# Attention beside a state-space layer: VectorE's exponential tiles copied in pairs, its single score tiles on zero-padded keys, and riders that open steps by columns

## The chip, the core and the metric

The kernel runs on one core of one Trainium2 chip. The metric is the device time of one execution in microseconds (us). TensorE is called PE, its weight loads PEld, VectorE DVE, ScalarE ACT, GpSimd POOL and SyncE (which issues most DMAs) SP, as in the profile.

## The reference

Two independent layers are computed on their own inputs of 2048 x 640, and their outputs stand side by side. Layer B, attention with 32 heads that share one key and one value head of 20 columns, carries most of the work:

```python
q = (x @ wq).reshape(B, S, H, Dh).transpose(0, 2, 1, 3)      # S 2048, D 640, H 32, Dh 20
k, v = x @ wk, x @ wv                                          # one key and value head for all
scores = einsum("bhqd,bkd->bhqk", q, k) * Dh ** -0.5
b = einsum("bhqk,bkd->bhqd", softmax(scores), v).transpose(0, 2, 1, 3).reshape(B, S, H * Dh) @ wo
# layer A: a diagonal state-space layer, complex state of 640
Bu = einsum("bld,pd->blp", x + 0j, B_bar)
for t in range(L): h = Lam_bar * h + Bu[:, t]                  # hs
a = 2 * einsum("bld,dp->blp", hs, Cmat).real + x * Dskip
out = concatenate([a, b], -1)
```

## The kernel before

**Tiles.** A block is 512 queries of four heads; there are 32 blocks. A block has 64 score tiles, one for each of 16 key groups of 128 keys (`kc`) and each of its four heads (`j`), so 2048 tiles in all (`NTILE`). A score tile is 128 keys by 512 queries in PSUM. Its exponential goes to SBUF in bf16, and a value product then multiplies it with 128 x 32 padded values (20 value columns and one of ones, which gives the softmax denominator). There is no pass for a maximum: a row in the padded query carries a bound.

**Two shapes on PE.** A score contracts over at most 32 rows, so it uses a quarter of the array's rows (`32*128` in the profile). Up to four such matmuls on four row groups, one for each head, run beside each other. I call them a row step. A value product contracts over 128 keys into 32 columns (`128*32`); four of them on four column groups, again one for each head, run beside each other: a column step. PE's instruction stream alternates between a stretch of one row step and a stretch of one to five column steps.

**Two ways to an exponential.** Most tiles go to ACT: PE fills two or three 512-column banks of one of two PSUM slots (`SC0`, `SC1`, three banks each), and ACT reads them in one `ACTIVATE` of 1024 or 1536 columns (L1530). The others go to DVE. Where ACT takes two banks of a slot, the third holds one DVE tile ("own" tile); further DVE tiles ("single" or lone tiles, `MB<-QT,KT`) go to a spare bank. DVE's exponential is made from bits: its first pass (L867, `BIG<-SC` or `BIG<-MB`) turns the score into the int16 bit pattern of a bf16 power of two, and three further copies of these 512 words, moved by 32, 64 and 96 (`SHIFTS`), are made from the first one by integer addition (POOL's `INT64_ADD`, L1858, or DVE's `TENSOR_SCALAR` on `BIG<-BIG`). The sum of the four, each with its own scaled values (`VS`), approximates the exponential. So a DVE tile needs four value products where an ACT tile needs one. Copies are made for two tiles at a time, the same shift of each, between any two of 20 (later 41) buffers of 512 words (`dhold`, `two`).

**Background.** All else on PE, the query projections, the state-space layer and the output products, is fed between these steps as column steps. A background product can also be a rider: four row pieces of it, each placed in the row group that a row step leaves free (`board`, L810). A rider opens a new step only where more than `KEEP_C` steps of the task are left.

**What sets the order.** The kernel is written by a planner in Python. Sources for each engine offer operations with priorities, a list schedule picks among them with assumed durations, and the result is a fixed instruction order for each engine with semaphores. A table (`STAGES`) sets priorities and limits anew as the count of tiles grows, `SHARE` limits DVE's part of the tiles. The order on the chip is therefore fixed; only waits vary. After a block's 64 tiles, its sums leave one PSUM bank (`pvsb<-MB`, L1925), and the reciprocals of the denominators pass through DRAM (L1980: `dn`, `rc`).

Of the kernel before, what the change touches and what calls it, by code (L numbers as in the profile page):

```python
# [445 lines left out]

class Holder:
# [20 lines left out]
class Build:  # L468
# [6 lines left out]
    MORE = 21  # L475
# [55 lines left out]
    def shared(self):  # L531
# [10 lines left out]
        shares["WO"] = ["qc"]  # L542
        shares["WOt"] = [f"BT{i}_{c}" for i in range(2) for c in range(NC)]
# [3 lines left out]
    SPREAD = 18.658  # L547
    SEEDS, REPLAYS = (169732,), 12
# [47 lines left out]
    def alloc(self, o):  # L596
# [49 lines left out]
        self.dn = sb(o, "dn", [64, 2, 32], BF16)  # L646
        self.rc = sb(o, "rc", [64, 2, 32], BF16)
# [165 lines left out]
    def board(self, op, used):  # L813
# [5 lines left out]
        for r in self.rides:  # L819
# [26 lines left out]
            return  # L846

# [22 lines left out]
    def program(self):  # L870
# [16 lines left out]
        self.dhold = [Holder(i) for i in range(self.NDS)]  # L887
# [9 lines left out]
        self.outs = 0  # L897
# [9 lines left out]
        self.s.spawn(self.more())  # L907
        self.free_banks.remove(self.pvbank)
# [32 lines left out]
    KEEP, KEEP_Q = 4200.0, 4  # L941
# [500 lines left out]
    def rules(self):  # L1442

        while self.stages and self.stages[0][0] <= self.tile_n:
# [7 lines left out]
        (0, {'STAY': 1.2, 'PAUSE': 500.0, 'pe': 192.807, 'dve': 150.0, 'KEEP_C': 3, 'OPEN': 1, 'PATIENCE': 2500.0, 'MARGIN':  # L1452
            648.138, 'WAITING': 2, 'REFILL': 905.623, 'SPARE': 148.045, 'LAG': 162.255, 'SOON': 3981.867, 'EARLIER': 3, 'LATER':
            7, 'AHEAD': 10, 'CAP': 3, 'ROOM': 4, 'ALONE': 1.397, 'TASK': 0.95, 'PV': 2.034, 'EV': 0.52, 'P1': 0.5, 'COPY': 0.569,
            'COPY1': 0.792, 'P1OWN': 0.391, 'PVEV': 0.2, 'SCARCE': 8, 'BACKLOG': 9, 'GRACE': 55.439, 'SHARE': 0.281, 'MISC_FIRST':
            0}),
        (250, {'STAY': 1.357, 'pe': 198.49, 'WAITING': 3, 'SPARE': 136.396, 'LAG': 190.385, 'SOON': 2730.774, 'EARLIER': 4,
            'ALONE': 2.237, 'PV': 1.984, 'COPY': 0.522, 'COPY1': 0.897, 'PVEV': 0.209, 'GRACE': 21.699, 'SHARE': 0.29}),
        (500, {'STAY': 1.083, 'pe': 192.807, 'PATIENCE': 2175.307, 'MARGIN': 696.79, 'SPARE': 163.248, 'LAG': 230.582, 'SOON':
            3202.285, 'EARLIER': 5, 'ALONE': 2.657, 'TASK': 0.989, 'PV': 1.9, 'P1': 0.475, 'COPY': 0.554, 'P1OWN': 0.406, 'PVEV':  # L1460
            0.2, 'SCARCE': 6, 'BACKLOG': 7, 'SHARE': 0.301}),
        (850, {'STAY': 1.2, 'PAUSE': 1035.401, 'dve': 185.73, 'PATIENCE': 2500.0, 'MARGIN': 765.584, 'WAITING': 2, 'REFILL':
            766.143, 'SPARE': 136.396, 'LAG': 240.378, 'SOON': 2255.472, 'EARLIER': 4, 'ALONE': 1.449, 'TASK': 0.95, 'PV': 1.889,
            'EV': 0.544, 'COPY': 0.57, 'PVEV': 0.259, 'BACKLOG': 9}),
        (1200, {'STAY': 0.876, 'PAUSE': 500.0, 'dve': 233.993, 'MARGIN': 696.79, 'REFILL': 905.623, 'LAG': 230.879, 'SOON':
            2154.193, 'ALONE': 2.13, 'PV': 1.756, 'EV': 0.506, 'COPY1': 0.9, 'PVEV': 0.2, 'BACKLOG': 8}),
        (1600, {'STAY': 1.2, 'PAUSE': 897.677, 'pe': 196.33, 'dve': 185.73, 'KEEP_C': 2, 'PATIENCE': 2150.555, 'WAITING': 3,
            'REFILL': 962.106, 'SOON': 2730.774, 'EARLIER': 5, 'AHEAD': 9, 'CAP': 2, 'ALONE': 1.525, 'PV': 1.9, 'COPY': 0.522,
            'PVEV': 0.309, 'BACKLOG': 7}),
    )  # L1470

    def fill_now(self, op, i, n):
# [6 lines left out]
        if s.t >= op.due or not self.can_d() or len(self.d_free()) < len(self.SHIFTS):  # L1479
            return True  # L1480
# [98 lines left out]
    def want_own(self):  # L1579
        if self.tile_n >= NTILE - self.LAST or self.d_count + 1 > self.SHARE * (self.tile_n - 16) or self.behind():  # L1580
            return False
        if sum(1 for o in self.firsts if o.start is None) >= self.WAITING:
            return False
        self.firsts = [o for o in self.firsts if o.start is None]
        return len(self.d_free()) > len(self.SHIFTS) - 1
# [100 lines left out]
    def can_d(self):  # L1686
# [5 lines left out]
        if b > self.pv_b and len(self.d_free()) < self.ROOM + min(self.due_copies(), self.CAP):  # L1692
            return False
# [5 lines left out]
    def due_copies(self):  # L1699
        return sum(len(d[2]) for d in self.d_open if d[3] <= self.pv_b)  # L1700

    def want_d(self, taken=0, own=0):
        s = self.s
        if self.tile_n >= NTILE - self.LAST or self.d_count + taken + own + 1 > self.SHARE * (self.tile_n - 16):
# [3 lines left out]
        return len(self.d_free()) > taken + own + len(self.SHIFTS) - 1  # L1708

    def d_source(self):  # L1710
# [9 lines left out]
        return Op("pe", [], self.mmt(512), prio=self.ALONE, mode="S", load=128.0, hook=hook)  # L1720
# [8 lines left out]
    def task_prio(self):  # L1729
        return self.TASK if self.started else 3  # L1730
# [10 lines left out]
    def fill_d(self, op, m, bank=None):  # L1741
# [6 lines left out]
        h = self.d_free()[0]  # L1748
        self.d_count += 1
        b, kc, j = self.score(op, m, bank.tensor, bank)  # L1750
        n = len(self.SHIFTS)
        h.taken, h.left, h.users = True, n, []
        key = f"DR{h.index}"
        first = self.dve(self.ts(self.dr(h.index), bank.ap, 16256.0, 0.0, ALU.add, ALU.max), 645, deps=[op],
# [5 lines left out]
        self.d_open.append([h, first, list(range(1, n)), b, kc, j])  # L1760
        self.d_left[b, j] += n - 1
        self.pv_entry(b, kc, j, 0, h, first)
# [3 lines left out]
    def pv_entry(self, b, kc, j, k, h, op):  # L1766
        self.pvq[b][j].append((self.VS[:, k], kc, self.dr(h.index, BF16), f"DR{h.index}", op, h, "VS"))
# [5 lines left out]
    def two(self, x):  # L1773
        a, b = (self.dr_at[i] for i in x)
        return bass.AP(tensor=self.BIG, offset=a, ap=[[self.BIG.shape[1], 128], [b - a, 2], [1, 512]])

    def more(self):
# [3 lines left out]
        self.dhold += [Holder(self.NDS + i) for i in range(self.MORE)]  # L1781
# [4 lines left out]

    def copy_source(self):

        s = self.s
        can = [d for d in self.d_open if d[1].end is not None and s.seen(d[1], "dve") <= s.t]  # L1790
        if not can:
            return None
        n = len(self.d_free())
        if n < 1:
            return None
        if sum(len(d[2]) for d in can) < self.BACKLOG and not (can[0][3] == self.pv_b and self.pv_filled[self.pv_b] == self.pv_need[self.pv_b]):
            return None
        k = can[0][2][0]
        two = [d for d in can if k in d[2]][:2 if n >= 2 else 1]
        if self.short(two):  # L1800
            two = two[:1]
        one = len(two) == 1
        if one and any(d[1].end is None or d not in can for d in self.d_open):
            prio = self.COPY1
        else:
            prio = self.COPY
        if can[0][3] == self.pv_b != LASTB and self.pv_filled[self.pv_b] == self.pv_need[self.pv_b]:
            prio = self.CLOSE
        return Op("dve", [], 210 if one else 342, prio=prio, port=True, hook=lambda op: self.copy(op, k, two))

    def short(self, two):

# [860 lines left out]
```

## Time and profile before

| | before |
|---|---|
| median of 3 runs (lowest, highest) | 697.5 us (696.67, 699.1) |
| span of the profiled execution, first to last instruction | 695.9 us |
| PE busy, share of the span | 683.2 us, 98% |
| ACT busy | 681.8 us, 98% |
| DVE busy | 637.0 us, 92% |
| POOL busy | 470.4 us, 68% |

Which of the runs was profiled isn't told, so the execution's own time stands for its span: 695.9 us, 0.8 us under the fastest run and 1.6 us under the median. "Busy" counts the time in which at least one instruction of the engine was under way; on ACT and PE instructions overlap, so that an instruction's mean duration is longer than the distance to the next one.

### The profile page before, as it was taken

The page shows a single profiled execution, that of the slowest core. Times are in us where ns is not written, and L with a number is a line of the kernel's source. Part 1 is how long each engine was busy: PE and PEld are TensorE (multiplying, and loading weights), DVE is VectorE, ACT ScalarE, POOL GpSimd, SP SyncE. Part 2 cuts the span into 40 slices and gives each one's busy share as a digit, 9 for nine tenths or more (in the row PEclk, how much of TensorE's full clock was granted, in tenths as well). Part 3 has the DMA queues.
Part 4 walks back from the last instruction along what each step waited for, and adds up shares of the span by engine and source line. Part 5 has one row for each costly group of instructions (what it writes and reads, how often), then busy time and mean ns, then how long its engine had stood idle before and what let it go on. Part 6 is the DMA issues. An engine that isn't in the chain of part 4 may idle for free.

```text
span 695.9 us, 27390 instructions
## 1 busy us (share of the span) xinstructions
PE 683.2 (98%) x11488; PEld 250.6 (36%) x11490; DVE 637.0 (92%) x1243; ACT 681.8 (98%) x703; POOL 470.4 (68%) x796
## 2 busy tenths in 40 slices
PE   8999999999999999999999999999999999999998
PEld 5322332334334333333433333334333332343335
DVE  7899999999999889999999999999999999977795
ACT  7999999999999999999999999999999999999996
POOL 4256666564587668767778777676776767788880
DMA  9659641211130111102110101131000001110001
GB/s 217 175 127 187 139 103 39 62 26 32 30 94 13 32 27 27 35 21 29 44 26 22 28 27 28 35 58 20 13 15 12 20 15 36 37 29 22 21 15 41
DMA packets 77591, 34.48 MB, mean 50 GB/s; under 512 B 58350, under 2 KB 77470, under 8 KB 77470
## 3 DMA queue, kind: packets, MB, share of 16 engines
q1 hardware_dynamic: 76650, 32.57, 20.3%
q8 instruction: 92, 1.51, 0.9%
q10 hardware_dynamic: 820, 0.16, 0.1%
q14 instruction: 29, 0.24, 0.1%
HBM read 11.53 MB, written 9.75 MB: 31 GB/s over the span
## 4 chain that ended last, share of the span: by engine, by line
PE 56%; ACT 42%; DVE 1%; issue 0%
ACT PR L1530 41%; PE MB L1946 21%; PE MB L800 14%; PE SC L1626 10%; PE MB L810 8%; PE MB L730 1%; DVE BIG L867 1%; PE SC L1162 1%; PE SC L726 1%; PE MB L726 0%; ACT L2197 0%; PE SC L730 0%; DVE pvsb L1925 0%; PE MB L1279 0%; DVE QT L867 0%
## 5 line engine op out<-in xcount | busy, mean ns | idle before, releaser
L1530 ACT ACTIVATE PR<-SC 128x1024 bf16<-128x1024 f32 (+1 forms) x678 | 666.6, 1131 | 4.5 <-PE SC L1626 3.3
L1858 POOL INT64_ADD BIG<-BIG x761 | 458.1, 617 | 198.1 <-DVE BIG L867 54.7
L867 DVE TENSOR_SCALAR BIG<-SC 128x512 int16<-128x512 f32 x560 | 376.2, 684 | 38.7 <-PE SC L1626 33.1
L1946 PE MATMUL MB<-BIG,VS 128*32 128x512 bf16 (+1 forms) x2468 | 269.8, 376 | 1.2 <-DVE pvsb L1925 0.9
L1626 PE MATMUL SC<-QT,KT 32*128 32x512 bf16 (+1 forms) x2073 | 265.3, 378 | 4.4 <-ACT PR L1530 1.8
L1946 PE MATMUL MB<-PR,VP 128*32 128x512 bf16 (+1 forms) x1495 | 222.3, 378 | 0.1
L1626 PEld LDWEIGHTS SC<-QT,KT 32*128 32x128 bf16 x2073 | 67.3, 91 | 133.8 <-ACT PR L1530 77.1
L1946 PEld LDWEIGHTS MB<-BIG,VS 128*32 128x32 bf16 x2468 | 68.5, 95 | 65.5 <-issue 41.4
L1946 PEld LDWEIGHTS MB<-PR,VP 128*32 128x32 bf16 x1495 | 55.1, 94 | 45.8 <-issue 33.0
L867 DVE TENSOR_SCALAR BIG<-BIG 128x1024 int16<-128x1024 int16 (+1 forms) x136 | 52.3, 419 | 0.9 <-PE MB L1946 0.4
L800 PE MATMUL MB<-CA,W 128*32 128x320 bf16 (+2 forms) x992 | 51.4, 299 | 0.4 <-DVE BIG L2366 0.4
L810 PE MATMUL MB<-xaT,BT 32*128 32x256 bf16 x192 | 37.1, 273 | 0.0
L800 PE MATMUL MB<-CT,W 128*32 128x512 bf16 (+1 forms) x640 | 36.0, 302 | 0.6 <-issue 0.6
L800 PE MATMUL MB<-xaT,BA 128*32 128x256 bf16 x800 | 31.8, 275 | 0.0
L810 PE MATMUL MB<-diagD,xaT 32*128 32x128 bf16 x320 | 31.3, 217 | 0.0
L810 PEld LDWEIGHTS MB<-diagD,xaT 32*128 32x128 bf16 x320 | 17.7, 92 | 29.1 <-ACT PR L1530 17.7
L800 PEld LDWEIGHTS MB<-CA,W 128*32 128x32 bf16 x992 | 22.8, 96 | 14.2 <-issue 5.7
L800 PE MATMUL MB<-xaT,BT 128*32 128x256 bf16 x608 | 26.2, 274 | 0.0
L2133 DVE CAST stg<-MB 128x512 bf16<-128x512 f32 x35 | 23.8, 680 | 1.8 <-PE MB L800 1.1
L862 DVE TENSOR_TENSOR prod<-MB,tab 128x1024 bf16<-128x1024 f32 x20 | 24.3, 1215 | 0.2
L867 DVE TENSOR_SCALAR BIG<-MB 128x512 int16<-128x512 f32 x35 | 23.8, 679 | 0.6 <-PE MB L1626 0.6
L2406 DVE TENSOR_TENSOR_SCAN g<-sc,hst,prod 128x256 bf16<-128x256 f32 x30 | 22.5, 749 | 0.0
(178 smaller groups left out, 502.4 us busy)
## 6 DMA issues: line engine op xcount, KB each, us to landing
out_dram<-stg SPq DMA_DIRECT2D x33, 128.0 KB, 2.0
qd<-BIG SPq DMA_DIRECT2D x20, 128.0 KB, 2.1
QT<-qd SPq DMA_DIRECT2D x28, 80.0 KB
OP<-pvsb SPq DMA_DIRECT2D x105, 20.0 KB
rdP<-recs SPq DMA_DIRECT2D x105, 20.0 KB
lbd<-BA SPq DMA_DIRECT2D x5, 320.0 KB, 2.7
CT<-in_B_x_dram SPq DMA_DIRECT2D x2, 640.0 KB, 5.3
BA<-in_A_B_re_dram SPq DMA_DIRECT2D x1, 800.0 KB, 7.5
```

The costliest lines, as they stand in the source:

```text
L726: r = e.matmul(out[32 * j:32 * j + 32], lhsT=lhsT[:, 32 * j:32 * j + 32], rhs=rhs, start=start, stop=stop, tile_position=(0, 32 * j), skip ...
L730: return lambda e: e.matmul(out, lhsT=lhsT, rhs=rhs, start=start, stop=stop, **kw)
L800: x = e.matmul(out[32 * j:32 * j + 32], lhsT=lhsT[:, 32 * j:32 * j + 32], rhs=rhs, start=start, stop=r.end is tag, tile_position=(0, 32 * ...
L810: return lambda e: e.matmul(out, lhsT=lhsT[at], rhs=rhs[at], start=start, stop=r.end is tag, tile_position=(32 * row, 0), skip_group_check ...
L862: return lambda e: e.tensor_tensor(out, a, b, op)
L867: return lambda e: e.tensor_scalar(out, a, s1, s2, op0=op0, op1=op1)
L1530: ex = self.act(lambda e: e.activation(dst, t[:, 0:512 * n], ACT.Exp, scale=1.0 / UNIT), 0.8333 * 512 * n + 64, table="exp", deps=[op], re ...
L1626: r = e.matmul(out[:, bank.off + lo:bank.off + lo + n], lhsT=p.KT[32 * j:32 * j + 32, 128 * c:128 * c + 128], rhs=p.QT[32 * j:32 * j + 32, ...
L1858: op.fns.append(lambda e: e.int64_add(words(dst), words(src), add))
L1946: r = e.matmul(bank.tensor[32 * j:32 * j + 32, bank.off + at:bank.off + at + n], lhsT=v[:, c, 0:32], rhs=rhs[:, lo:lo + n], start=first an ...
L2133: ev = self.dve(lambda e: e.tensor_copy(st, bank.ap), 645, deps=[prev], reads=[bank.key], writes=[key], prio=self.EV, gate=(lambda: last.e ...
L2406: o = self.dve(lambda e, ri=ri, init=init: e.tensor_tensor_scan(p.g[:, u, ri, :], rdec, p.prod[:, 1, 0, ri, :], init, ALU.mult, ALU.add), ...
```

## The change

The diff rewrites the handling of DVE's tiles and retunes the planner's table.

- **Pairs.** Buffers are held as pairs of neighbours (10, later 20 pairs). Two DVE tiles share a pair. The pair's first copy (shift 32) is one operation on 1024 words; the other two (64 and 96) are one operation on 2 x 1024 words, since adding 64 to the tiles and to their first copy gives both (`CHAIN`, `step_of`).
- **Lone tiles on zero-padded keys.** After the last row of queries is projected, POOL zeroes four strips of 384 columns in `BIG` and SP copies 32 rows of the last three key groups into each (`lone_keys`). A single tile of these key groups is then scored by four `128*32` matmuls that contract over all 128 rows, three quarters of them zeros in the keys (`lone`, `MB<-QT,BIG`), a column step.
- **Riders.** A rider opens a step where at least `RIDE_N` columns of the task's other steps are left (654 to 2600, by stage), in place of a count of steps.
- **Also.** The reciprocal works on 128 x 16 in place of 64 x 32; a task of the output waits until `wo` has landed and a unit of the state-space layer until its inputs nearly have; tasks get a lower priority unless one is due (`EASY`); `STAGES` has 31 rows in place of 6, with another seed.

```diff
-    MORE = 21
+    MORE = 20
...
-            if best is None and rows and len(r.steps) > self.KEEP_C and len(r.open) < self.OPEN:
+            if best is None and rows and len(r.open) < self.OPEN and self.width(r.steps) >= self.RIDE_N:
...
+        if self.lone_at() is not None:
+            return Op("pe", [], self.mmt(512, 4), prio=self.ALONE2, mode="C", load=512.0, hook=self.lone)
...
+            op.fns += [lambda e, i=i: e.matmul(out[32 * i:32 * i + 32, bank.off:bank.off + 512], lhsT=keys[:, at + 32 * i:at + 32 * i + 32],
+                                               rhs=p.QT[:, b % 12, :], start=True, stop=True, tile_position=(0, 32 * i),
+                                               skip_group_check=True) for i in range(4)]
...
+    def step_of(self, d, free, eng):
+
+        s = self.s
+        if d.first is not None and len(d.todo) == 2 and len(d.tiles) == 2 and self.CHAIN:
+            if d.first[1].end is None or s.seen(d.first[1], eng) > s.t:
+                return None
+            if free > 1 and not self.short(d, 4):
+                return (2, 3)
+        if free < 1 or self.short(d, len(d.tiles)):
+            return None
+        return (d.todo[0],)
...
-        two = [d for d in can if k in d[2]][:2]
-        if len(two) < 2 or self.short(two):
+        can = [x for x in self.ready_pairs("pool") if len(x[0].tiles) == 2]
+        if not can:
             return None
...
+            op.fns.append(lambda e: e.int64_add(b.bitcast(I64), a.bitcast(I64), by * 0x0001000100010001))
...
-        o = self.dma(lambda e: e.dma_start(p.dn[:, slot, :], sums.rearrange("j (s n) -> (j s) n", n=32)), 4096, dn, land=self.LATE_DMA, deps=[o],
+        o = self.dma(lambda e: e.dma_start(p.dn[:, slot, :], sums.rearrange("j (s n) -> (j s) n", n=16)), 4096, dn, land=self.LATE_DMA, deps=[o],
...
     def o_ready(self, qb):
         blks = range(NC if qb < NQB - 1 else 1)
+        if not self.s.done([self.wo_op]):
+            return False
```

How the two programs' instructions count out (the order as built; "full columns" means 512):

| instructions | before | after |
|---|---|---|
| ACT exponentials of 1024, of 1536 columns | 579, 98 | 552, 120 |
| DVE first passes (own from SC, single from MB) | 560 + 35 = 595 | 535 + 48 = 583 |
| DVE copies `BIG<-BIG`, of 512 words (15 absolute values among them) / of 2 tiles / of 4 | 24 / 127 / 0 | 18 / 17 / 9 |
| POOL `INT64_ADD` on `BIG`, of 2 tiles / of 4 | 761 / 0 | 284 / 277 |
| PE stretches of row steps, of them with a score step for ACT | 674, 672 | 668, 666 |
| row stretches with all four row groups in use / with three | 360 / 301 | 297 / 353 |
| PE column steps, in units of four matmuls of full columns | 1649 | 1683 |
| of these: value products / lone tiles / fillers on zeros (L730, `MB<-KT,VZ`) | 958 / 0 / 18.5 | 949 / 22 / 25.5 |
| background in column steps, same units | 673 | 687 |
| single tiles as row matmuls of full columns | 31 | 26 |

The PE order at a place in the second half, before: three score matmuls (own tile among them), the single DVE tile on the fourth row group, then value products.

```order
L1626 MATMUL SC<-QT,KT 128x512 x3
L1626 MATMUL MB<-QT,KT 128x512
L1946 MATMUL MB<-PR,VP 32x512
L1946 MATMUL MB<-BIG,VS 32x512
L1946 MATMUL MB<-PR,VP 32x512 x2
L1946 MATMUL MB<-BIG,VS 32x512
```

And after, at a like place, where the score lines are L1677, the value products L2106 and the lone tile L1909:

```order
L1677 MATMUL SC<-QT,KT 128x512 x3
L1909 MATMUL MB<-QT,BIG 32x512 x4
L2106 MATMUL MB<-BIG,VS 32x512 x2
L2106 MATMUL MB<-PR,VP 32x512
L2106 MATMUL MB<-BIG,VS 32x512
```

The single tile has moved from the row step into the column stretch, as a step of its own. POOL's queue before, all additions over two tiles (`2x256` are two buffers apart, `512` two neighbours, in 64-bit words):

```order
L1858 ISA BIG<-BIG 128x2x256 x3
L1858 ISA BIG<-BIG 128x512 x2
L1858 ISA BIG<-BIG 128x2x256 x2
L1858 ISA BIG<-BIG 128x512 x2
L1858 ISA BIG<-BIG 128x2x256 x3
```

And after, the additions over two tiles and over four in turn:

```order
L2007 ISA BIG<-BIG 128x512
L2007 ISA BIG<-BIG 128x2x512
L2007 ISA BIG<-BIG 128x512
L2007 ISA BIG<-BIG 128x1024
L2007 ISA BIG<-BIG 128x512
L2007 ISA BIG<-BIG 128x2x512
```

What took three POOL instructions for two tiles takes two, the second of them twice as wide. DVE's queue before had copies between its first passes:

```order
L867 TENSOR_SCALAR BIG<-SC 128x512
L867 TENSOR_SCALAR BIG<-BIG 128x1024
L867 TENSOR_SCALAR BIG<-SC 128x512 x2
L1980 RECIPROCAL rc<-dn 64x32
L867 TENSOR_SCALAR BIG<-SC 128x512
L2133 CAST stg<-MB 128x512
```

And after, in the middle of the program, mostly none:

```order
L883 TENSOR_SCALAR BIG<-SC 128x512
L2140 RECIPROCAL rc<-dn 128x16
L878 TENSOR_TENSOR W<-prod 128x2x256
L883 TENSOR_SCALAR BIG<-SC 128x512 x2
L878 TENSOR_TENSOR prod<-prod 128x512
L883 TENSOR_SCALAR BIG<-SC 128x512 x3
```

The copies have left DVE for POOL's wider instructions.

More of the change, by code (lines that the diff above doesn't have):

```diff
@@ L1799, in copy_source @@
[L1799 to L1807, printed above, removed]
+        d, ks = can[0]
+        closing = d.b == self.pv_b and self.pv_filled[self.pv_b] == self.pv_need[self.pv_b]
@@ L1836, in act_source @@
             return None
[L1837 to L1858 removed]
+        can = self.ready_pairs("act")
```

330 lines of the change are left out of this document (226 added, 104 removed).

## The prediction

> **What bounds the kernel now.** I read the page's engine line and chain first, then the groups by shape, then the window from the first exponential to the last.
>
> ```profile
> PE 683.2 (98%) x11488; PEld 250.6 (36%) x11490; DVE 637.0 (92%) x1243; ACT 681.8 (98%) x703; POOL 470.4 (68%) x796
> PE 56%; ACT 42%; DVE 1%; issue 0%
> 18.40:687.00 668.60, 661.20 (x11210) 237.77 (x11212) 620.83 (x1183) 665.93 (x677) 462.26 (x769) 1.00 0.19 44
> L1530 ACT ACTIVATE PR<-SC 128x1024 bf16<-128x1024 f32 x579 | 544.7, 1068 | 4.3 <-PE SC L1626 3.3 <-PE MB L1626 0.3 <-PE MB L1946 0.2
> L1530 ACT ACTIVATE PR<-SC 128x1536 bf16<-128x1536 f32 x98 | 141.6, 1505 | 0.1
> ```
>
> PE and ACT are both at 98%, and the chain of waits is shared between them (56% and 42%). The third line is the stretch that matters, 668.6 us from the first exponential to the last; its columns are PE, PEld, DVE, ACT and POOL busy, then the granted clock, 1.00. Ahead of it lie 18.4 us and behind it 695.9 - 687.0 = 8.9 us. ACT's recorded idle time, 4.5 us in that stretch, understates its waiting, because an `ACTIVATE` that waits overlaps its predecessor in the record. So I take the distance between starts where ACT doesn't wait. These four rows are single instructions of its timeline:
>
> ```profile
> 456.19 1.04 ACT L1530 ACTIVATE PR<-SC 128x1024 bf16<-128x1024 f32 x1
> 465.22 1.17 ACT L1530 ACTIVATE PR<-SC 128x1024 bf16<-128x1024 f32 x1
> 167.86 1.53 ACT L1530 ACTIVATE PR<-SC 128x1536 bf16<-128x1536 f32 x1
> 175.84 1.19 ACT L1530 ACTIVATE PR<-SC 128x1024 bf16<-128x1024 f32 x1
> 456.19 9.29 ACT L1530 ACTIVATE PR<-SC 128x1024 bf16<-128x1024 f32 x10
> ```
>
> Ten exponentials of 1024 lie between 456.19 and 465.22 (last row): 0.903 us each. Six of 1536 lie between 167.86 and 175.84: 1.330 us each. Without any wait ACT needs 579 x 0.903 + 98 x 1.330 = 522.8 + 130.3 = 653.2 us of the 668.6. Its whole slack is 15.4 us, 2.3%.
>
> PE in the same way, from a place where nothing seems to hold it (only starts matter):
>
> ```profile
> 300.34 0.39 PE L1626 MATMUL SC<-QT,KT 32*128 32x512 bf16 x3
> 300.66 0.40 PE L1946 MATMUL MB<-BIG,VS 128*32 128x512 bf16 x4
> 300.88 0.38 PE L1946 MATMUL MB<-PR,VP 128*32 128x512 bf16 x1
> 301.21 0.39 PE L1626 MATMUL SC<-QT,KT 32*128 32x512 bf16 x3
> 301.53 0.39 PE L1946 MATMUL MB<-PR,VP 128*32 128x512 bf16 x1
> 302.30 0.39 PE L1626 MATMUL SC<-QT,KT 32*128 32x512 bf16 x3
> ```
>
> A column step takes 0.22 us (300.66 to 300.88), a stretch of two 0.55 (300.66 to 301.21) and of three 0.77 (301.53 to 302.30). So a column stretch costs 0.11 plus 0.22 for each step, and a row step 0.32, of which 0.1 is again the turn to the other shape. Row step and two column steps make 0.87, under ACT's 0.903; with three they make 1.09, and ACT waits. So the two engines take turns as the bound from one exponential to the next.
>
> **The change, part by part.**
>
> *ACT.* 27 exponentials of 1024 go and 22 of 1536 come, since DVE takes 583 tiles in place of 595: -27 x 0.903 + 22 x 1.330 = -24.4 + 29.3 = **+4.9 us**, on the path wherever ACT is the bound.
>
> *PE, lone tiles.* 22 of them become column steps, 22 x 0.22 = +4.8 us. What they cost as row matmuls shows here:
>
> ```profile
> 453.17 0.39 PE L1946 MATMUL MB<-BIG,VS 128*32 128x512 bf16 x4
> 453.49 0.39 PE L1626 MATMUL SC<-QT,KT 32*128 32x512 bf16 x3
> 453.50 0.38 PE L1626 MATMUL MB<-QT,KT 32*128 32x512 bf16 x1
> 453.81 0.39 PE L1946 MATMUL MB<-BIG,VS 128*32 128x512 bf16 x1
> ```
>
> The single tile starts 0.01 us behind its three neighbours on the fourth row group, and the next stretch starts 0.32 after the row step: it was free. In the order all 31 stand in a stretch that has a score step anyway. At worst a single tile comes alone after the row step and costs another 0.32. I take free.
>
> *PE, riders.* The background needs 687 - 673 = 14 more column units, as pieces that rode on free row groups do so no longer: +3.1 us. The 12 fewer DVE tiles save 9 units of value products, -2.0. Six fewer turns of shape and row steps save 6 x (0.32 + 0.11) = -2.6. The fillers' 7 units more (+1.5) are issued where PE has nothing else, so I leave them out. PE's sum is 4.8 + 3.1 - 2.0 - 2.6 = **+3.3 us** (+4.8 with the fillers). The turn is also where a rule speaks for the change.
>
> ```profile
> PEld SC L1626 <- ACT PR L1530: 77.1, 189, 0.7
> PEld SC L1626 <- DVE BIG L867: 31.3, 77, 0.7
> PEld SC L1626 <- issue: 14.7, 42, 0.5
> ```
>
> These are the idle times of the weight queue ahead of score steps: 0.41 us each where ACT came last, 0.41 where DVE came last, 0.35 where nothing held it but the turn itself. The Trainium skill ("TensorEngine Tiling (Array Packing)", Key Properties) says that a change of tiling mode drains TensorE; the trace agrees, at 0.1 us a turn. By that rule alone, had the 22 tiles stood in stretches of their own, they would have cost 0.32 + 0.11 = 0.43 each, the new shape would bring 22 x (0.22 - 0.43) = -4.6 in place of +4.8, and PE's sum would be -6.1 (ACT's 4.9 would stand); the order has no such stretches, so the saving isn't there to be had. The same page's Performance Considerations take contractions of 32 rows as a case for row tiling, which speaks against the zero-padded keys, and the rows above agree.
>
> *DVE.* The pairs take its copies away and the shorter reciprocal some more:
>
> ```profile
> L867 DVE TENSOR_SCALAR BIG<-SC 128x512 int16<-128x512 f32 x560 | 376.2, 684 | 38.7 <-PE SC L1626 33.1
> L867 DVE TENSOR_SCALAR BIG<-BIG 128x1024 int16<-128x1024 int16 x127 | 50.2, 427 | 0.9 <-PE MB L1946 0.4
> L1980 DVE RECIPROCAL rc<-dn 64x32 bf16<-64x32 bf16 x30 | 10.0, 333 | 0.0
> L1858 POOL INT64_ADD BIG<-BIG x761 | 458.1, 617 | 198.1 <-DVE BIG L867 54.7 <-PE MB L1946 22.1 <-DVE g L2406 19.3
> ```
>
> Copies over two tiles 110 x 0.427 = -47; nine over four tiles, each between one and two of these, +3.8 to +7.7, I take +6; first passes 12 x 0.684 = -8; half the reciprocal's work between 0 and -10, I take -5 since half of its columns remain. DVE falls by some 54 us, to 583 (84%). That is off the path, except where DVE came last ahead of a score step: 77 x (0.41 - 0.35) = 4.6 us at most. ACT waits just as long there, so most of these would only change their releaser. I take **-1.2**, and keep 0 and -4.6 as ends.
>
> *POOL.* 284 additions over two tiles at 0.617 make 175 us. The 277 over four aren't in the trace: not under one of 0.617, not over two of them, so 171 to 342 us. The two memsets below, 526 ns for 512 columns and 1805 for 2048, leave a fixed part of about (4 x 526 - 1805) / 3 = 100 ns; by that a four-tile addition takes 2 x 0.617 - 0.1 = 1.13 us, 313 us in all, and POOL's copying rises to 488 us from 458. It had 198 us of idle time ahead of these instructions, which hides that and the four new memsets (narrower than QT's at 526 ns).
>
> ```profile
> L1014 POOL MEMSET QT<- 128x512 bf16 x10 | 5.3, 526 | 7.1 <-DVE M L866 4.7 <-DVE VS L862 1.8
> PEld MB L1946 <- POOL BIG L1858: 10.2, 45, 0.3
> L1017 POOL MEMSET VS<- 128x2048 bf16 x1 | 1.8, 1805 | 0.0
> SPq L1982 <- DVE rc L1980: 92.5, 25, 7.2
> SPq L1973 <- DVE BIG L867: 80.1, 20, 9.6
> ```
>
> If the cover went, a value product would find its copy late by up to one more 0.617. Today PE waits for POOL 45 times for 0.23 us, which is the ordinary gap. I take nothing; the upper end, one full 0.617 at each of 31 block ends, is 19 us, since one PSUM bank holds the sums of one block at a time.
>
> *SP.* Four loads more for the keys, and 60 small transfers in twice the rows. SP waits with an instruction for DVE for many us (last two rows) while nothing on PE stops for it; its output transfers are as many as before. Nothing, unless a copy to the keys is late, and then single tiles keep the old shape. The new conditions for `wo` and the inputs can only move background work.
>
> *Sum.* ACT-bound stretches grow by 4.9, PE-bound ones by 3.3 to 4.8. The engines are used in turn, so I take ACT's 4.9 with DVE's -1.2 against it: +3.7. From the profiled execution 695.9 + 3.7 = 699.6 us of span; the median lies 1.6 above the span, so **701.2 us**.
>
> **Rivals.**
>
> *The waits shrink by more than the work grows (faster).* The new table has 31 stages, and DVE is freer, so single and own banks come free sooner. ACT's slack is 15.4 us; if half of it went, 695.9 + 4.9 - 7.7 = 693.1 of span and 694.7 us. It decides from a slack of 15.4 - 4.9 = 10.5 us downward. For it: the slack is made of many small misfits of the order (0.87 against 0.903 against 1.09), which another order could fit better. Against it: PE has no more than 668.6 - 661.2 = 7.4 us without a matmul under way, and gets more work too. The floor without any wait is 18.4 + 658.1 + 8.9 = 685.4 of span.
>
> *No difference.* The slack shrinks by about what is added: 697.5, within 2.1 us either way. A difference of 0.3%, 2.1 us, is about what this kernel's runs can tell.
>
> *POOL's wide copies come late (slower still).* The pair has to wait for its second tile, then for a copy of twice the width; if a third of the upper end's 19 us falls on the path, 701.2 + 6.3 = 707.5. It decides once POOL's queue is longer than the value products' reserve at a block's end. Against it: POOL's 198 us idle. The Trainium skill ("SBUF — State Buffer", Who interferes with whom) says that GpSimd and a two-port VectorE instruction exclude each other for a whole instruction, so a wider POOL copy would hold VectorE longer as well; the trace agrees as far as POOL waited 54.7 us for VectorE's L867, and no run here shows the reverse.
>
> **How the numbers follow.** Forecast (699.6 to 705.7) 0.47; faster 0.28; no difference 0.15; late copies 0.10. So slower holds 0.57 against 0.28 and 0.15. The likeliest case is 701.2. For 8 in 10 the range leaves out half of the late copies and somewhat less than half of the faster case, those in which more than half of the slack goes: 692 to 706.5. The likeliest case's own range is 699.6, where no difference begins, to 705.7, where ACT's 4.9 and PE's 3.3 would both count in full and DVE's part for nothing.
>
> **What the changed profile would show.** ACT: 552 and 120 exponentials at 0.903 and 1.330 between starts, and a stretch from first to last of 671 to 674 us. If it is under 668, the slack fell below 10.5 us and the first rival holds. PE: `MB<-QT,BIG` with a start 0.22 us ahead of the next column step. DVE: under 600 us busy. POOL: the mean of four-tile additions between 0.62 and 1.23 us; if over 1.23, or if PE's waits for POOL rise from 10.2 to over 20 us, the third rival holds. The prediction would be wrong if the order of steps matters more than their number.

## The result and the profile after

| | before | after |
|---|---|---|
| median (lowest, highest), 4 runs each | 697.45 us (696.67, 699.1) | 702.93 us (702.28, 703.12) |
| ratio to before, 95% interval | | 1.0073 [1.0058, 1.0088] |
| the profiled execution, and its span | 695.9 us of span | 703.12 us, 701.2 us of span |

The changed kernel is 0.7% slower, some 5.1 us by the ratio. First the answers to the prediction's first fence: the engine line, the chain by engine, the window from the first exponential to the last (PE, PEld, DVE, ACT, POOL busy, then clock and DMA), and ACT's two groups.

```profile
PE 686.9 (98%) x11567; PEld 252.9 (36%) x11567; DVE 612.8 (87%) x1124; ACT 686.3 (98%) x698; POOL 470.6 (67%) x600
ACT 56%; PE 40%; DMA 2%; DVE 1%; issue 0%
18.25:692.52 674.27, 664.57 (x11297) 240.10 (x11298) 597.41 (x1066) 670.34 (x672) 462.50 (x573) 1.00 0.18 44
L1581 ACT ACTIVATE PR<-SC 128x1024 bf16<-128x1024 f32 x552 | 522.1, 1084 | 5.4 <-PE SC L1677 5.0 <-PE MB L2106 0.2
L1581 ACT ACTIVATE PR<-SC 128x1536 bf16<-128x1536 f32 x120 | 173.5, 1518 | 0.2 <-PE MB L2106 0.2
```

The stretch grew from 668.6 to 674.3 us, which is all of the loss between these two executions; the head is 0.15 shorter and the tail 8.7 in place of 8.9. ACT and PE stand at 98% as before, and the chain has moved from PE towards ACT. DVE lost 24 us of busy time, and the span grew all the same.

Busy time says little about two engines whose instructions overlap in the record, so I add up what each had to do in that stretch. For ACT that is the count of exponentials by the distance between starts without a wait (0.903 and 1.330 us; the quartiles of these distances are the same in both traces). For PE I take every step by the usual shortest distance of its kind to the next step (the fifth percentile over both traces: a full column step to a column step 0.215 us, column to row and row to column 0.320, narrower ones less). Depending on how neighbouring matmuls are put together into steps, the difference in PE's work comes out between 5.1 and 5.6 us.

| from the first exponential to the last, us | before | after | difference |
|---|---|---|---|
| length | 668.6 | 674.3 | +5.7 |
| ACT's work | 653.2 | 658.1 | +4.9 |
| ACT's rest | 15.4 | 16.2 | +0.8 |
| PE's work | 635.5 | 640.6 | +5.1 |
| PE's rest | 33.1 | 33.7 | +0.6 |

Both engines were given about 5 us more to do, and neither waits less than before. The two rests come from single executions, though, and the four runs of the kernel before spread over 2.4 us. That is the first reading of the loss; the experiments ask whether it holds as a cause.

A lone tile in its new shape, four matmuls on zero-padded keys (first column start, second duration, us):

```profile
325.32 0.39 PE L1677 MATMUL SC<-QT,KT 32*128 32x512 bf16 x3
325.64 0.40 PE L1909 MATMUL MB<-QT,BIG 128*32 128x512 bf16 x4
325.86 0.39 PE L2106 MATMUL MB<-BIG,VS 128*32 128x512 bf16 x4
```

It starts 0.22 us ahead of the next column step. Of the 22, 16 are followed by a column step at once and take 0.215 to 0.227 us, one more only after 0.38; the other five stand last in their stretch.

The waits (in order: total us, times, longest), the weight queue ahead of score steps and of value products, and DVE's first passes ahead of their scores:

```profile
PEld SC L1677 <- ACT PR L1581: 108.5, 264, 1.2
PEld SC L1677 <- DVE BIG L883: 27.0, 66, 1.1
PEld SC L1677 <- issue: 16.3, 46, 0.4
DVE BIG L883 <- PE SC L1677: 58.6, 166, 2.6
PEld MB L2106 <- POOL BIG L2007: 11.8, 49, 0.7
```

DVE comes last ahead of a score step 66 times in place of 77, ACT 264 times in place of 189. The 11 steps that no longer wait for DVE can be at most a small part of the 75 that now wait for ACT. The time that the pairs took off DVE shows again as waiting for PE: the first passes' idle time behind score steps went from 33.1 (the group's row before) to 58.6 us.

DVE's and POOL's groups, those that changed:

```profile
L883 DVE TENSOR_SCALAR BIG<-SC 128x512 int16<-128x512 f32 x535 | 361.1, 686 | 65.0 <-PE SC L1677 58.6 <-PE MB L1677 1.8
L883 DVE TENSOR_SCALAR BIG<-MB 128x512 int16<-128x512 f32 x48 | 32.6, 678 | 1.2 <-PE MB L1909 0.8 <-PE MB L1677 0.2
L883 DVE TENSOR_SCALAR BIG<-BIG 128x1024 int16<-128x1024 int16 x17 | 7.6, 444 | 0.4
L883 DVE TENSOR_SCALAR BIG<-BIG 128x2048 int16<-128x2048 int16 x9 | 6.3, 703 | 0.5 <-PE MB L2106 0.3
L2140 DVE RECIPROCAL rc<-dn 128x16 bf16<-128x16 bf16 x30 | 7.2, 241 | 0.0
L2007 POOL INT64_ADD BIG<-BIG x561 | 456.8, 823 | 201.4 <-DVE BIG L883 47.6 <-DVE g L2566 24.2 <-PE MB L2106 18.6
```

POOL's additions over two and over four tiles share the last row; single ones of its timeline tell them apart:

```profile
302.72 0.61 POOL L2007 INT64_ADD BIG<-BIG  x1 [4.36 <-DVE BIG L883]
303.70 1.04 POOL L2007 INT64_ADD BIG<-BIG  x1 [0.37 <-DVE prod L878]
```

A four-tile addition takes 1.04 us, so POOL copies as long as before (456.8 and 458.1 us).

### The profile page after: what moved, and what is told of

It reads as the page before. It is cut to its first block, busy times and chain, and to the rows that moved or that the text cites. A ratio compares the mean times of both kernels' runs of the same rounds, so it can differ in the third digit from the quotient of the medians.

```text
span 701.2 us, 27176 instructions
## 1 busy us (share of the span) xinstructions
PE 686.9 (98%) x11567; PEld 252.9 (36%) x11567; DVE 612.8 (87%) x1124; ACT 686.3 (98%) x698; POOL 470.6 (67%) x600
## 4 chain that ended last, share of the span: by engine, by line
ACT 56%; PE 40%; DMA 2%; DVE 1%; issue 0%
ACT PR L1581 56%; PE MB L2106 13%; PE MB L809 11%; PE SC L1677 8%; PE MB L819 4%; DMA mrep<-mab 2%; PE MB L739 1%; PE SC L1179 1%; PE SC L735 0%; DVE BIG L883 0%; DMA mcol<-mrep 0%; PE MB L735 0%; ACT L2357 0%; PE SC L739 0%; DVE prod L878 0%
## 5 line engine op out<-in xcount | busy, mean ns | idle before, releaser
L2007 POOL INT64_ADD BIG<-BIG x561 | 456.8, 823 | 201.4 <-DVE BIG L883 47.6
L883 DVE TENSOR_SCALAR BIG<-SC 128x512 int16<-128x512 f32 x535 | 361.1, 686 | 65.0 <-PE SC L1677 58.6
L1677 PE MATMUL SC<-QT,KT 32*128 32x512 bf16 (+1 forms) x2064 | 263.1, 377 | 6.6 <-ACT PR L1581 4.7
L2106 PE MATMUL MB<-BIG,VS 128*32 128x512 bf16 (+1 forms) x2408 | 263.8, 377 | 0.4 <-issue 0.4
L2106 PE MATMUL MB<-PR,VP 128*32 128x512 bf16 (+1 forms) x1510 | 215.5, 378 | 0.0
L1677 PEld LDWEIGHTS SC<-QT,KT 32*128 32x128 bf16 x2064 | 66.6, 91 | 158.7 <-ACT PR L1581 108.5
L2106 PEld LDWEIGHTS MB<-BIG,VS 128*32 128x32 bf16 x2408 | 66.1, 95 | 64.7 <-issue 42.0
L2106 PEld LDWEIGHTS MB<-PR,VP 128*32 128x32 bf16 x1510 | 53.5, 94 | 41.1 <-issue 29.0
L819 PE MATMUL MB<-xaT,BT 32*128 32x256 bf16 x176 | 34.0, 273 | 0.0
L883 DVE TENSOR_SCALAR BIG<-MB 128x512 int16<-128x512 f32 x48 | 32.6, 678 | 1.2 <-PE MB L1909 0.8
L819 PE MATMUL MB<-diagD,xaT 32*128 32x128 bf16 x320 | 31.3, 217 | 0.8 <-ACT PR L1581 0.8
L2566 DVE TENSOR_TENSOR_SCAN g<-sc,hst,prod 128x256 bf16<-128x256 f32 x30 | 24.4, 818 | 0.1
L809 PE MATMUL MB<-BIG 128*32 128x512 bf16 x300 | 22.6, 382 | 0.0
```

The source lines that it names most:

```text
L809: x = e.matmul(out[32 * j:32 * j + 32], lhsT=lhsT[:, 32 * j:32 * j + 32], rhs=rhs, start=start, stop=r.end is tag, tile_position=(0, 32 * ...
L819: return lambda e: e.matmul(out, lhsT=lhsT[at], rhs=rhs[at], start=start, stop=r.end is tag, tile_position=(32 * row, 0), skip_group_check ...
L883: return lambda e: e.tensor_scalar(out, a, s1, s2, op0=op0, op1=op1)
L1677: r = e.matmul(out[:, bank.off + lo:bank.off + lo + n], lhsT=p.KT[32 * j:32 * j + 32, 128 * c:128 * c + 128], rhs=p.QT[32 * j:32 * j + 32, ...
L2007: op.fns.append(lambda e: e.int64_add(b.bitcast(I64), a.bitcast(I64), by * 0x0001000100010001))
L2106: r = e.matmul(bank.tensor[32 * j:32 * j + 32, bank.off + at:bank.off + at + n], lhsT=v[:, c, 0:32], rhs=rhs[:, lo:lo + n], start=first an ...
```

## The experiments

Theory W: the order after the change asks for more work of ACT and PE, the two engines at the bound, the waits stay as they are, and the work is the loss. Theory O: added work would be absorbed by the waits, and the loss comes from the new order or from a new wait. Theory P, the prediction's third rival: POOL's wide copies come late. All kernels below keep the instruction order of the kernel that they start from, so that nothing is planned anew; only a_lone_moved moves 18 matmuls and, where one would come too early, the first pass that reads it. Ratios go against the kernel before, run in turn with them on the same chip; differences in us are differences of ratios by 698 us, with the intervals combined by their squares.

| kernel | changed by | median, us | ratio to before, 95% interval | against its own start, us |
|---|---|---|---|---|
| after | | 702.93 | 1.0073 [1.0058, 1.0088] | |
| b_act | before, ACT +4.2 us | 699.84 | 1.0018 [1.0009, 1.0028] | +1.3 ± 0.7 |
| b_pe | before, PE +3.2 to 3.7 | 702.63 | 1.0066 [1.0048, 1.0083] | +4.6 ± 1.2 |
| b_both | before, both | 702.66 | 1.0064 [1.0049, 1.0079] | +4.5 ± 1.0 |
| b_act_short | before, ACT -4.8 | 697.24 | 0.9982 [0.9973, 0.9991] | -1.3 ± 0.6 |
| b_pe_short | before, PE -3.0 | 696.60 | 0.9970 [0.9959, 0.9981] | -2.1 ± 0.8 |
| a_act_short | after, ACT -4.7 | 701.53 | 1.0039 [1.0027, 1.0051] | -2.4 ± 1.3 |
| a_pe_short | after, PE -3.0 | 701.79 | 1.0046 [1.0030, 1.0062] | -1.9 ± 1.5 |
| a_both_short | after, both | 698.16 | 1.0004 [0.9995, 1.0013] | -4.8 ± 1.2 |
| a_lone_moved | after, 18 lone tiles on row steps | 703.41 | 1.0068 [1.0052, 1.0084] | -0.3 ± 1.5 |
| a_lone_inplace | after, lone tiles as rows in place | 702.52 | 1.0067 [1.0054, 1.0080] | -0.4 ± 1.4 |
| a_pool_split | after, POOL +61 | 709.72 | 1.0168 [1.0152, 1.0184] | +6.6 ± 1.5 |
| a_pool_short | after, POOL -41 | 702.57 | 1.0064 [1.0046, 1.0083] | -0.6 ± 1.7 |

### Adding the work to the kernel before

Small copies between ACT's exponentials, and value products on zeros as extra column steps, 45 and 15 of them, spread evenly.

```diff
+                x = Op("act", [lambda e: e.activation(p.tscr[:], p.lift[:, 2:3], ACT.Copy)], 100.0)
...
+                op.fns[:0] = [lambda e, j=j: e.matmul(bank.tensor[32 * j:32 * j + 32, bank.off:bank.off + 512], lhsT=p.VZ[:], rhs=p.KT[:, 0:512],
+                                                      start=False, stop=False, tile_position=(0, 32 * j), skip_group_check=True) for j in range(4)]
```

> The kernel before in its own order, with 45 one-column ACT copies put evenly between its exponentials, ahead of the next exponential's wait; at the 0.11 us that two small ACT instructions stand apart they are 4.9 us of ACT work, as much as the change adds. Theory W (the work: the change is slower because its order asks more of ACT and PE, and the waits stay as they are): 700.4 to 702.4 us, 3 to 5 over before. Theory O (the order: the added work alone would vanish in ACT's 15.4 us of slack, and the change is slower because its order fits worse): under 699 us.

> The kernel before in its own order, with 15 column steps on zeros put evenly among the value products, 0.22 us each, 3.3 us of PE work. Theory W: 699 to 700.8 us, 1.5 to 3.3 over before. Theory O: under 698.5 us.

> The kernel before with both additions, 4.9 us of ACT work and 3.3 us of PE work. Theory W: 702 to 704.5 us, about the 702.9 of the changed kernel. Theory O: under 700 us.

One such copy on ACT's timeline of b_act:

```profile
299.60 1.03 ACT L1546 ACTIVATE PR<-SC 128x1024 bf16<-128x1024 f32 x1
300.50 0.21 ACT L558 ACTIVATE tscr<-lift 128x1 f32<-128x1 f32 x1
300.59 14.34 ACT L1546 ACTIVATE PR<-SC 128x1024 bf16<-128x1024 f32 x15
```

It holds ACT for 0.093 us from start to start (300.50 to 300.59, rounded), whatever its recorded 0.21, so 45 of them are 4.2 us. Of these 1.3 came out at the end: short of theory W's 3 to 5, and by this difference within the 1.5 that theory O left. PE's 15 steps are 3.2 us at 0.215 each; the sum over steps puts the same 15 at 3.7 us in b_pe and 4.3 in b_both, so it is good to about 1 us. They cost 4.6 us, their length or more and over the 1.5 to 3.3 that was expected. Both additions together, within theory W's range, cost no more than PE's alone. So the kernel before is held by PE more than by ACT, and 4.2 us of ACT and 3.2 to 4.3 us of PE give it +4.5 us, close to what the change lost.

### Taking work away, from both kernels

Every exponential behind the first 200 tiles leaves out 10 columns of its last tile, or every value product behind the first of a block 8 of its 512 columns, or both.

```diff
+        self.n_seen = getattr(self, "n_seen", 0) + n
+        cut = 512 * n - (10 if self.n_seen > 200 else 0)
+        dst = p.PR.rearrange("p a b -> p (a b)")[:, 512 * h.index:512 * h.index + cut]
...
+                n -= 8 if n == 512 and not first else 0
```

> The changed kernel in its own order, with ScalarE's work made shorter: every exp behind the first 200 key tiles leaves out the last 10 columns of its last tile (10 x 0.83 ns each, some 600 exps, about 5.0 us less work; those columns keep what an earlier exp left). Theory W (the order of the changed kernel asks for 4.9 us more of ScalarE, and ScalarE is its bound): it comes 3 to 5 us under the changed kernel, 698 to 700, about where the kernel before stands. Theory O (the exps' waits set the end, whatever the work): 1.5 us or less under it, 701.5 or more.

> The changed kernel in its own order, with TensorE's work made shorter: every value product that is not the first of its block streams 504 of 512 columns (8 columns at 0.417 ns, about 890 steps of four side by side, about 3.0 us less work; the last 8 columns of each sum lack those products). Theory W with ScalarE as the bound of the changed kernel, as the moved lone tiles suggest: 0 to 1.5 us under the changed kernel, 701.5 to 703. If TensorE is the bound after the change too: 2 to 3 us under it, about 700.

> The kernel before in its own order, with ScalarE's work made shorter in the same way (the last 10 columns of every exp behind the first 200 key tiles left out, about 5.0 us). The added copies cost 0.2 to 0.6 of their length here, so TensorE holds the exps back: 0.5 to 2 us under the kernel before, 695.5 to 697.5. If ScalarE were its bound as well: 3 to 5 us under it, about 693.

> The kernel before in its own order, with TensorE's work made shorter in the same way (504 of 512 columns in the value products behind the first of a block, about 3.0 us). TensorE is its bound: 2 to 3 us under the kernel before, 694.5 to 696. If ScalarE and TensorE hold each other up at single places only: under 1.5 us.

> The changed kernel in its own order with both cuts at once: 10 columns less in the last tile of every exp behind the first 200 key tiles (4.8 us of ScalarE), 504 of 512 columns in the value products behind the first of a block (3.0 us of TensorE). The single cuts gave 0.0034 and 0.0027 of the time before, 2.4 and 1.9 us. If each engine holds the other up at places of its own, the two add up: 4.3 us under the changed kernel, 699.0 to 700.0, a ratio of 1.001 to the kernel before. If both cuts shorten the same waits: 2.5 to 3 us, 700.5 or more. If one engine takes over as soon as the other is cut: 5.5 us or more, 698 or less.

On ACT a cut exponential starts the next one 0.008 us sooner (0.895 for 0.903, 1.322 for 1.330), 579 times in the changed kernel and 585 times in the one before, so 4.7 and 4.8 us. ACT's cut gives 2.4 us in the changed kernel and 1.3 in the one before; PE's gives 1.9 and 2.1. By these differences a_act_short and a_pe_short each fell between their two expectations; the cuts of the kernel before came as expected. So neither engine is the bound by itself, before or after. ACT's part may have grown with the change, as the chain has it, but the two intervals of ACT's cuts overlap. With both cuts the changed kernel is where the kernel before is, 1.0004 [0.9995, 1.0013], and 4.8 us are near the sum of the single cuts, 4.3, which speaks for each engine holding the other up at places of its own; the interval, 3.6 to 6.0, excludes cuts that shorten the same waits, but not the 5.5 us or more of one engine taking over from the other. Its engine line and chain:

```profile
PE 683.5 (98%) x11565; PEld 253.0 (36%) x11567; DVE 612.9 (88%) x1124; ACT 682.8 (98%) x698; POOL 470.4 (68%) x600
ACT 49%; PE 45%; DMA 3%; DVE 1%; SPq 1%; issue 0%
```

The changed kernel has kept its order, its pairs, its wide copies and its DVE queue there; only 4.7 us of ACT and 3.0 us of PE are gone, and with them the loss. Together with b_both, which gives the kernel before about the same loss by adding such work, this bears theory W out from both sides. Theory O fails in its first half: the kernel before absorbs most of ACT's added work but none of PE's, and 7.7 us taken from the two engines of the changed kernel give 4.8 back. Its second half, that the new order costs or gains something by itself, is not tested by these runs; it can only be bounded by how well the added work accounts for the loss (below).

### The lone tiles

The change's own column steps, undone in two ways: 18 of the 22 as row matmuls on the free row group of the next score step (the other four find none), or all 22 as row matmuls where they stand.

```diff
+        op.fns = [lambda e: e.matmul(out[:, bank.off:bank.off + 512], lhsT=p.KT[32 * j:32 * j + 32, 128 * kc:128 * kc + 128],
+                                     rhs=p.QT[32 * j:32 * j + 32, b % 12, :], start=True, stop=True, tile_position=(32 * j, 0))]
```

> The changed kernel with 18 of its 22 lone tiles taken out of the column stretches and put, as row matmuls on the real keys, on the free row group of the next score step; all else stays in its order. PE loses 18 column steps of 0.22 us, 4.0 us. Theory W: 699 to 701 us, 2 to 4 under the changed kernel's 702.9. Theory O, or the tiles as a thing that only fills PE's gaps: 702 to 703.5 us. If the later score holds up VectorE or the next fill: over 703.5 us.

> The changed kernel in its own order, with the 22 lone tiles at their places as single 32-row matmuls instead of zero-padded column steps: each then lies as a row between two column steps and costs two more turns, 22 x 0.21 us = 4.6 us more of TensorE at just these places. If TensorE's time at these places is on the path, as the prediction's sum had it (0.6 to 1 of it by what the other cuts gave): 2.8 to 4.6 us over the changed kernel, 706 or more. If ScalarE is the bound there, as the moved lone tiles suggest: 0 to 1 us, 703 to 704.5.

Moved, the tiles take 3.9 us off PE by the sum over steps, and the time stays: theory W's 2 to 4 us under the changed kernel did not come. The chain of a_lone_moved shows what may be a part of the reason:

```profile
PE 57%; ACT 33%; DVE 5%; DMA 3%; issue 0%; POOL 0%; POOLq 0%
```

DVE stands at 5% in place of 1%. A lone tile that is scored later reaches DVE later: DVE's first passes wait 4.1 us for the moved tiles, 9 times, where they waited 0.8 us for the lone tiles of the changed kernel. That this is what eats up PE's 3.9 us is not shown, but it makes the run a poor test of the steps' own price. The second run was to add 4.6 us of turns at the same places, and didn't: 18 of the 22 have a row step right ahead or behind and join it, and PE's sum fell by 2.4 us. In the trace, 12 of these 18 row stretches still last 0.45 to 0.65 us, not much less than row step and zero-padded step together (0.32 + 0.22), so little of that sum was saved in fact; the time didn't move either. So the shape of the lone tile is worth nothing that can be measured here, one way or the other. What a step at these places costs by itself, these two runs leave open, and theory W rests on work that was added and taken away evenly over the kernel, not on the change's own steps.

### GpSimd's copies

The wide additions split into two of two tiles, or all additions 140 columns short of each pair.

```diff
+                one = [(self.wide_at([x], n), self.wide_at([y], n)) for x, y in zip(free, src)]
+                op.fns += [lambda e, o=o, i=i: e.int64_add(o.bitcast(I64), i.bitcast(I64), by * 0x0001000100010001) for o, i in one]
...
+            if all(h.index in self.full for h in free):
+                a, b = self.wide_at(src, n, 140), self.wide_at(free, n, 140)
```

> The changed kernel in its own order, with each of GpSimd's 277 four-tile additions made as two of two tiles: 277 x (2 x 0.588 - 1.013) = 45 us more of GpSimd, 457 to about 502 us. If the copies' time on GpSimd is on the path (the prediction's third rival): 2 to 5 us over the changed kernel, 705.5 or more. If not: 0 to 1 us. By the way VectorE's operations on SBUF: if they wait for the end of one GpSimd addition, their mean falls back (prod<-prod 526 to some 440 ns) because each is shorter; if they wait by GpSimd's total, it stays or grows.

> The changed kernel in its own order, with GpSimd's copies made shorter: behind the first copy into each buffer an addition leaves out the last 140 columns of each pair of tiles (884 of 1024, 1768 of 2048; at 0.415 ns a column of each pair some 0.058 us a pair, 838 pairs, about 45 us less of GpSimd, 457 to about 412; those columns keep an older copy). The split additions cost 6.6 us for 65 us more of GpSimd. Theory P (the wide copies come late as the change stands, and a part of its 5.2 us is theirs): 2 to 5 us under the changed kernel, 698 to 701. Theory W (the change's loss is ScalarE's and TensorE's work, and GpSimd has slack up to about where it stands): 0 to 1 us under it, a ratio of 1.006 or more to the kernel before.

The groups of additions and the chain in a_pool_split (L2009 are the split ones):

```profile
L2009 POOL INT64_ADD BIG<-BIG x554 | 344.3, 635 | 46.9 <-POOL BIG L2011 13.3 <-DVE g L2570 4.2 <-DVE BIG L883 3.8
L2011 POOL INT64_ADD BIG<-BIG x284 | 177.8, 630 | 101.3 <-DVE BIG L883 33.4 <-DVE CT L878 14.7 <-DVE diagD L882 11.5
PE 58%; ACT 23%; POOL 7%; DVE 6%; issue 3%; DMA 2%; POOLq 0%; DVEq 0%
```

And in a_pool_short its group, and PE's waits for it:

```profile
L2010 POOL INT64_ADD BIG<-BIG x561 | 415.5, 748 | 241.2 <-DVE BIG L883 59.5 <-PE MB L2110 26.8 <-DVE g L2570 25.4
PEld MB L2110 <- POOL BIG L2010: 10.2, 41, 1.0
```

The two groups overlap where one addition follows another; POOL's engine line rose from 470.6 to 531.3 us, by 61. With that POOL enters the chain with 7% and the kernel loses 6.6 us, more than the 2 to 5 expected; with 41 us less it gains nothing that can be measured. So theory P is not borne out for the change as it stands: POOL's copies cost it nothing, or at most the 2.3 us of that interval. But they have little room left: somewhere between 471 and 531 us of busy time they come onto the path, at an engine that is idle for a quarter to a third of the span.

## Why the prediction was right, point by point

- **The result.** 701.2 was forecast, 702.9 came; slower, within the range and within the likeliest case's own range (699.6 to 705.7). The span came to 701.2 in place of 699.6.
- **ACT, +4.9 us.** 552 and 120 exponentials at unchanged distances: the work rose by 4.9 as worked out. The stretch was forecast at 671 to 674 us and is 674.3.
- **PE, +3.3 (+4.8 with fillers).** The sum over steps gives +5.1, nearer to the count with the fillers. I left them out because they are issued where PE has nothing else; they stood in the count all the same.
- **The lone tiles' price.** The column step takes 0.22 us as forecast. That the row matmul was free holds for PE: of the 18 row steps that took one in a_lone_moved, 17 last 0.32 to 0.33 us. It isn't shown for the whole kernel, which gains nothing from it, with DVE waiting longer for these tiles.
- **DVE, -1.2 on the path: the term with no sign of it in the traces.** The waits with DVE as the last fell by 4.3 us (31.3 to 27.0), those with ACT as the last rose by 31.4 (77.1 to 108.5). By the prediction's own measure, what lies over the 0.35 us of a plain turn, DVE's part fell by some 0.7 us and ACT's rose by some 4. ACT's rest didn't fall by 1.2 but rose by 0.8. These 2.0 us, less the 0.4 by which head and tail are shorter, are the span's miss of 1.6. That is arithmetic between two single executions, and within the spread of the runs; no run gave DVE its copies back, so that its relief was worth nothing isn't shown.
- **DVE's busy time, 583: wrong, 612.8.** The test "under 600" failed. The copies lost 38 us (forecast 41), the first passes 6 (8), the reciprocal 2.8 (5). But DVE's instructions on SBUF grew longer, next section, by 7.6 us over five groups. And instructions that follow each other without a wait overlap in the record: the sum of DVE's durations fell by 42 us (719.5 to 677.7), the busy time by 24; a likely reason is that the queue now stops for PE more often between them.
- **POOL, 488: wrong, 456.8.** The four-tile addition takes 1.04 us, not 1.13, and the two-tile one 0.61: a fixed part of 2 x 0.61 - 1.04 = 0.18 us in place of the 0.10 that two memsets gave. "Nothing on the path" was right: PE's waits for POOL are 11.8 us in 49 places (10.2 in 45), and a_pool_short gains nothing.
- **The way of adding up.** I let ACT's 4.9 stand for the sum, since the engines are used in turn. That gave the right size by a wrong split, and so in part by luck: PE's term was dropped, and ACT's taken at its full length. The evenly spread additions and cuts give 0.3 to 0.5 us of time for each us of ACT and 0.6 to 1.4 for each of PE; with both moved together it is 4.5 / 8.5 = 0.53 (b_both, 0.61 with 3.2 us for PE) and 4.8 / 7.7 = 0.62 (a_both_short) for each us of either. The change's 4.9 + 5.1 = 10.0 us come to 5.3 to 6.2 by these, to some 4 to 8 with the intervals of the two runs; 5.1 was measured. The lone tiles, 4.8 us of PE by the prediction, gave nothing back when they were moved, and in the kernel before PE's part alone makes all of b_both's loss, so how the 5.1 us divide is open.
- **The rivals.** The waits didn't shrink: ACT's rest is 16.2 us, where 10.5 was the point of decision. That there is no difference is excluded by the interval, [1.0058, 1.0088]. Late copies aren't seen: PE's waits for POOL stay under the 20 us that the prediction set, and a_pool_split shows that they need more POOL time than the change asks for. One reading in that rival is wrong: the 54.7 us that POOL waited for VectorE's L867 are waits for the first pass whose output the addition reads, and say nothing about shared ports.
- **The doubt stated last,** that the order might matter more than the number of steps: the numbers account for the loss within a few us, so an effect of the order of that size can't be excluded. What stays open is the share of single parts. Pairs, lone tiles and riders can't be taken back singly without planning a new order, and which of them made the planner give DVE 12 tiles fewer, which is where ACT's 4.9 us come from, was not tried.

## What to carry to other kernels

Where two engines stand at 98% and take turns, don't count on a third one's saved time: here 24 us less of VectorE went with a slower kernel. Count what the new order asks of each of the two; here somewhat over half of the sum of both differences came out as time, in one kernel and its variants. Price a wait that names the freed engine near nothing unless the other engine's work falls as well. To learn which engine holds a kernel, cut a few columns from its instructions with the order fixed: that told more here than busy shares or the chain, neither of which says what a microsecond is worth. And test the change's own instructions too: evenly spread ones needn't cost the same.

## What the runs showed of the hardware

VectorE's instructions on SBUF took longer beside GpSimd's wider additions. Before, then after, the same three groups (the last number ahead of the second bar is the mean in ns):

```profile
L862 DVE TENSOR_TENSOR W<-prod 128x512 bf16<-128x512 bf16 x20 | 8.9, 444 | 0.0
L862 DVE TENSOR_TENSOR prod<-prod 128x512 bf16<-128x512 bf16 x20 | 8.6, 431 | 0.0
L867 DVE TENSOR_SCALAR W<-CT,sc 128x1280 bf16<-128x1280 bf16 x5 | 3.1, 628 | 0.0
```

```profile
L878 DVE TENSOR_TENSOR W<-prod 128x512 bf16<-128x512 bf16 x20 | 10.6, 529 | 0.0
L878 DVE TENSOR_TENSOR prod<-prod 128x512 bf16<-128x512 bf16 x20 | 10.5, 526 | 0.1
L883 DVE TENSOR_SCALAR W<-CT,sc 128x1280 bf16<-128x1280 bf16 x5 | 4.1, 819 | 0.0
```

Split by whether one of POOL's additions was under way: `prod<-prod` takes 408 ns before and 418 after where none was, and 443 before and 615 after where one was; `W<-prod` 416 and 415 without, 463 and 623 with (7 to 13 records each). One such pair on the timelines of the kernel after:

```profile
81.28 1.04 POOL L2007 INT64_ADD BIG<-BIG  x1 [0.66 <-DVE BA L878]
81.70 0.96 DVE L883 TENSOR_SCALAR W<-CT,sc 128x1280 bf16<-128x1280 bf16 x1
```

The `TENSOR_SCALAR` takes 0.96 us and ends at 82.66, 0.34 behind POOL's end at 82.32; the one of the five without an addition beside it takes 0.54. With the additions cut by 140 columns of a pair the overlapped `prod<-prod` take 480 ns and `W<-prod` 568. With the wide ones split, over all 20 of each, `prod<-prod` falls from 526 to 498 ns, less far than the 440 expected for a wait that ends with one addition. `W<-prod` goes from 529 to 573, but by one record alone: it lasted 2.60 us, through four additions that followed each other at once; the other 19 average 466. So shorter additions mean shorter waits for most, and additions in a row can hold an instruction longer than one would.

The Trainium skill ("SBUF — State Buffer", Who interferes with whom) says that VectorE in its two-port modes and GpSimd exclude each other: whichever issues first has their shared ports for its whole instruction, and the other waits. Which mode these instructions ran in no trace shows. The rows agree in the direction, and not in the size: after a full wait the `TENSOR_SCALAR` would have ended its own 0.54 us behind POOL's end, and it ended 0.34 behind. Here the five groups of VectorE that grew most took 7.6 us more. None of it shows on the path: in a_pool_short VectorE is busy for 605.3 us in place of 612.8, and the time moves by -0.6 ± 1.7 us.
